# Attention matmuls over all 128 rows of the array, and a third of w_spatial converted after attention

## The chip, the core and the metric

One core of a Trainium2 chip runs the whole kernel. The core has a matrix engine (TensorE; PE in the profile, its weight loads PEld), VectorE (DVE), ScalarE (ACT), GpSimd (POOL) and SyncE (SP), which issues most of the transfers. The engines run side by side, each through its own list of instructions in order, and wait for each other by semaphores. The metric is the device time of the kernel in microseconds (us).

## The reference

Two parts follow each other: a chunked attention, and a gated network whose gate mixes tokens. There are 4 batches, 8 heads, 768 tokens and 64 elements a head. Each chunk of 32 queries sees 8 memory keys and a window of 56 keys around it, 64 keys in all.

```python
for c in range(nc):                       # 24 chunks of 32 queries
    l_start = max(0, c_start - 16); r_end = min(S, c_end + 8)
    k_full = concatenate([mem_k, k[:, :, l_start:r_end]])
    v_full = concatenate([mem_v, v[:, :, l_start:r_end]])
    scores = scale * (q_c @ k_full.T)
    a = softmax(scores)
    out[:, :, c_start:c_end] = a @ v_full

x = out                                   # (4, 768, 512)
h = relu(x @ w_in)                        # 512 -> 1024
u, v = h[..., :512], h[..., 512:]
v_n = (v - mean(v)) / sqrt(var(v) + 1e-6)
v_s = einsum('ts,bsd->btd', w_spatial, v_n) + b_spatial
out = (u * v_s) @ w_out
```

## The kernel before

**Planner.** Each step is handed to `op` (line 40) with its engine, an assumed duration, what it reads and writes, and a rank. `Plan.order` (line 64) lays the steps out in an assumed time: of the steps that could start first, the lowest rank goes first. Each engine gets its steps in that order, and keeps to it on the chip. Names such as `big`, `st`, `uo` are rings of buffers; a new user waits until the oldest one's last reader is done. Transfers on SP wait in their order too.

**Attention.** A unit is 4 chunks (128 queries) of all 8 heads of a batch, 24 units in all, 6 a batch. Heads come in pairs: head pair t (four of them) has its first head (r = 0) in rows 0 to 63 of the 128 partitions and its second (r = 1) in rows 64 to 127, since a head has 64 elements. For unit i, `prep` (line 366, copy at 368) copies the keys on ACT from the loaded tile into one of two buffers `kmain`, in slots of 40 columns, where the last 8 hold the memory keys (`spread_keys`, line 372, on POOL at the start of each batch). `burst` (line 379) is a run of small matmuls on PE, all issued in line 382: for unit i the scores of queries and keys, and for unit i - 1 probabilities times values. For each head pair, chunk and head there is one matmul with 64 rows, 32 columns of weights (the queries of a chunk, or its probabilities) and 64 columns streamed. It occupies a tile of 64 by 32 of the array, so that eight matmuls of different tiles can be under way at once. The profile counts each of these 32-bit matmuls as two instructions, and as many weight loads. The result is the tile `sx`, two PSUM banks. After that follow the row maximum, subtraction, exponential and sum (`softmax`, line 425), the transpose of the probabilities (line 466), their copy `pT` (469), and for the unit before it the normalisation `xs` (418), its transpose `xt` (481) and the split into a high and a low part `x` (486, 490). Values lie in `vmain` (three unit buffers), with rows of memory values written by `spread_mem` (line 353). The last `x` carries the key `attended` (line 495).

**Input product.** `ffn_v` and `ffn_u` multiply `x` and `w_in`, both split in a high and a low part, by three matmuls each (lines 519 to 521). Their steps have later ranks than attention, so they fill PE between the bursts. Results go to DRAM (`vn_far`, `u_far`). `w_in` and `w_out` come as 64-bit numbers and are turned into 32-bit ones by `from_f64` (line 803: ACT 814 and 819, DVE 823 and 824, POOL 829).

**Second half.** `spatial` and `ffn_o` use seven products in place of eight (`product`, line 627, matmuls in line 679). For this `right_hand` (line 856) builds seven blocks of a weight matrix from its quarters: sums on POOL (line 871), high parts on ACT (843), low parts on POOL or DVE (847). `w_sp_pair(s)` (line 897) loads two row blocks of `w_spatial` into the ring `big` (four buffers) and builds one third of `wsp`. The three thirds are made during attention, at units 6, 10 and 14; the bias at unit 16. `w_out_pair` (line 886) loads `w_out` into the same ring with a rank of 200, and its blocks are built once the input product is done. The memory of attention is given back by `second_half` (line 596), when the first tile of the second half is made, and that of `w_in` by `third_part` (line 603).

Of the kernel before, what the change touches and what calls it, by code (L numbers as in the profile page):

```python
# [140 lines left out]
def tile_chunked_attention_gmlp(  # L141
# [68 lines left out]
    wsp = const.tile([P, 7, 2, HU, HT], F32R, name="wsp")  # L210
# [22 lines left out]
    vmain = values.tile([P, T, NV * UC, D], F32, name="vmain")  # L233
    NK = sizes["kT"]
    kmain = [values.tile([P, T, UC + 1, SLOT], F32, name=f"kmain{j}") for j in range(NK)]
    make_identity(nc, ident)
    nc.vector.memset(mhalf, -0.5)
# [79 lines left out]
    def v_of(i):  # L317
        o = (i % NV) * UC
        return vmain[:, :, o:o + UC]

    def load_v(i, seq=True, second="SP"):
        b, c0 = i // UB, (i % UB) * UC
        n = UC
        v4 = v_of(i).rearrange("p t c d -> p t (c d)")
        for r in range(2):
            p0 = r * D
# [26 lines left out]
    def spread_mem(i, eng, rank):  # L353
        b, o = i // UB, (i % NV) * UC
        for r in range(2):
            rows = slice(r * D + CH, r * D + SLOT)

            def spread(rows=rows):
                to, of = vmain[rows, :, o:o + UC], memv[rows, b].unsqueeze(2).broadcast_to([M, T, UC, D])
                if eng == "ACT":  # L360
                    nc.scalar.copy(to, of)
                else:
                    {"DVE": nc.vector, "POOL": nc.gpsimd}[eng].tensor_copy(to, of)
            op(eng, 2.6 if eng == "POOL" else 1.25, spread, r=[("memv", r)], w=[("vmem", i % NV, r)], rank=rank)

    def prep(i, rank):
        def keys():
            nc.scalar.copy(kmain[i % NK][:, :, :, 0:CH], k_of(i).rearrange("p t (c s) -> p t c s", s=CH))  # L368

        op("ACT", act(T * (UC + 1) * CH), keys, r=qk_keys(i, "k"), w=[("kmain", i % NK)], rank=rank)  # L370

    def spread_keys(i, rank):
        b = i // UB

        def spread():
            nc.gpsimd.tensor_copy(kmain[i % NK][:, :, 0:UC, CH:SLOT], memT[:, b].unsqueeze(2).broadcast_to([P, T, UC, M]))
        op("POOL", 0.3, spread, r=["memT"], w=[("kmem", i % NK)], rank=rank)

    def burst(i, rank, split=False):
# [4 lines left out]
        def go(what):  # L384
            if ("sx", i) not in t_:
                alloc("sx", i, [P, 2, 2, T, D], F32, psum=True)
            sx = t_["sx", i]
            tiles = [(t, c, r, slice(r * D, (r + 1) * D)) for t in range(T) for c in range(UC) for r in range(2)]
            if "s" in what:
                tq = q_of(i)  # L390
                kT = kmain[i % NK].rearrange("p t c s -> p t (c s)")
                for t, c, r, rows in tiles:
                    mm(sx[c * CH:(c + 1) * CH, r, 0, t], tq[rows, t, c * CH:(c + 1) * CH],
                       kT[rows, t, c * SLOT:c * SLOT + WIN])
            if "a" in what:
                pT, vt = t_["pT", i - 1], v_of(i - 1)
                for t, c, r, rows in tiles:
                    mm(sx[c * CH:(c + 1) * CH, r, 1, t], pT[rows, t, c * CH:(c + 1) * CH], vt[rows, t, c])
        whole = ("a" if i >= 1 else "") + ("s" if i < NU else "")
        for what in (whole if split else [whole]):  # L400
            reads, writes = [], []
            us = 0.4
            if "s" in what:
                reads += qk_keys(i, "q") + [("kmain", i % NK), ("kmem", i % NK)]
                writes.append(("sx", i, 0))
                us += 0.6
            if "a" in what:
                reads += [("pT", i - 1)] + v_keys(i - 1)
                writes.append(("sx", i, 1))
                us += 0.7  # L410
            op("PE", us, lambda what=what: go(what), r=reads, w=writes, rank=rank, tail=0.25)
        if i >= 1:
            j = i - 1

            def norm():
                xs = alloc("xs", j, [P, T, 2, D], F32)
                rec = t_["rec", j]
                nc.vector.tensor_tensor(xs.rearrange("p t r d -> p r t d"), t_["sx", i][:, :, 1],  # L418
                                        rec.rearrange("p t r -> p r t").unsqueeze(3).broadcast_to([P, 2, T, D]),
                                        op=ALU.mult)  # L420
# [4 lines left out]
    def softmax(i, rank):  # L425
        c0 = (i % UB) * UC

        def top():
            s = t_["sx", i][:, :, 0]
# [4 lines left out]
            mx = t_["mx", i] = small.tile([P, 2, T], F32, tag="mx", name="mx")  # L434
            nc.vector.tensor_reduce(mx, s, axis=AX.X, op=ALU.max)

        def sub():
            p = alloc("p", i, [P, T, 2, WIN], F32)
            nc.vector.tensor_tensor(p.rearrange("p t r w -> p r t w"), t_["sx", i][:, :, 0],
                                    t_["mx", i].unsqueeze(3).broadcast_to([P, 2, T, WIN]), op=ALU.subtract)  # L440
# [155 lines left out]
    def second_half():  # L596
        if "op" not in sb:
            attention.close()
            for name in ("vr", "op", "sm"):
                sb[name] = pool(name, bufs=sizes[name], side="right")  # L600
            ps["y"] = pool("ps_y", bufs=sizes["y"], space=PSUM, side="right")
# [106 lines left out]
    def spatial(b):  # L708
# [4 lines left out]
        def done(name, p, bank):  # L713
# [37 lines left out]
            elif name == "p3":  # L751
# [3 lines left out]
                lambda i, x, s: wsp[:, i, x, s], lambda i: [("wsp", s, i) for s in range(HU)], "DVE", True, done)  # L755
# [47 lines left out]
    def from_f64(name, src_, rank, load_rank, home):  # L803
# [7 lines left out]
        load(get, src_.bitcast(U32).rearrange("p (c w) -> p c w", w=2), w=[("big", big)], rank=load_rank, seq=True)  # L811
# [74 lines left out]
    def w_out_pair(c, rank, load_rank):  # L886
# [6 lines left out]
        (zu, ku), (zd, kd) = [from_f64(("wout", d), w_out[d * P:(d + 1) * P], rank, load_rank, True) for d in (c + 2, c)]  # L893
        end = [("fin", n) for n in range(count[0])]
        right_hand("wout", c, HN, halves(zu), halves(zd), [ku, *end], [kd, *end], dst, rank, "POOL", "DVE")

    def w_sp_pair(s, rank):
        raw = []
# [9 lines left out]
        right_hand("wsp", s, HT, u, d, ku, kd, lambda i, x: wsp[:, i, x, s], rank, "POOL", "POOL")  # L908


    def load_bias(rank):
# [7 lines left out]
        op("POOL", 0.8, clear, r=[("wsp", 2, 6)], w=[raw], rank=rank)  # L919
# [37 lines left out]
    for i in range(NU + 1):  # L957
# [13 lines left out]
        if i in (UB, UB + 4, UB + 8):  # L971
            w_sp_pair((i - UB) // 4, 10.0 * i + 15)
        if i == UB + 10:
            load_bias(10.0 * i)
    for b in range(B):
        for hf in range(2):
            for tt in range(hf * HU, (hf + 1) * HU):
                ffn_v(b, tt)
            for d in range(ND):
                ffn_u(b, hf, d)  # L980
    for c in range(2):
# [61 lines left out]
```

## Time and profile before

| | |
|---|---|
| three runs | 398.49, 399.73, 404.72 us; median 399.73 |
| the profiled execution | 404.88 us, its span 403.0 us |
| busy in the span | PE 365.8, PEld 334.4, DVE 272.7, ACT 190.7, POOL 151.8 us |
| mean granted clock of TensorE | 0.979 |
| instructions | 11801, of them 4972 matmuls and 4972 weight loads |

The span runs from the first to the last instruction of one execution. Busy time counts an engine's instructions, not its waits. In the rows of groups, after the bar stand the busy time in us, the mean time of one instruction in ns, and the idle time of the engine just before them with what ended it; "issue" means that the profile shows nothing that the engine waited for. In the timeline a row is the start, the length and the instruction, and idle time before it in brackets.

### The profile page before, as it was taken

How to read it: one execution, taken by the hardware profiler on the slowest of the kernel's cores; microseconds unless marked ns; L12 is line 12 of the kernel's file. 1: busy time of each engine (PE TensorE's matmuls, PEld its weight loads, DVE VectorE, ACT ScalarE, POOL GpSimd, SP SyncE). 2: the span in 40 equal slices, each digit the busy share in tenths (PEclk: the TensorE clock that was granted, in tenths of full speed). 3: DMA queues.
4: the chain of work that ended last, by engine and by line, in shares of the span. 5: the costliest groups of instructions: out<-in, count | busy, mean ns of one | idle time of the engine just before them, and what ended most of it. 6: DMA issues, size and time to landing. Idle time of an engine off the chain costs nothing.

```text
span 403.0 us, 11801 instructions
## 1 busy us (share of the span) xinstructions
PE 365.8 (91%) x4972; PEld 334.4 (83%) x4972; DVE 272.7 (68%) x462; ACT 190.7 (47%) x344; POOL 151.8 (38%) x151
## 2 busy tenths in 40 slices
PE   1587588799799999899999999999999999999986
PEld 0365478689689888698897989999999999999976
DVE  3577975376468676585859559967956884788473
ACT  4546544363346364253456234728344734453271
POOL 5323643561269058440113218560136033403510
PEclk9998889899989999999999999999999999999999
DMA  7987767835693877646582443832640544041004
GB/s 213 249 218 211 199 177 207 262 99 174 195 250 116 252 219 221 173 138 193 152 258 108 160 156 124 283 116 96 219 153 6 157 171 144 5 167 67 0 2 156
DMA packets 47368, 65.12 MB, mean 162 GB/s; under 512 B 4434, under 2 KB 38866, under 8 KB 47316
## 3 DMA queue, kind: packets, MB, share of 16 engines
q1 hardware_dynamic: 46900, 64.25, 52.6%
q8 instruction: 39, 0.64, 0.7%
q10 hardware_dynamic: 416, 0.13, 0.1%
q14 instruction: 13, 0.11, 0.1%
HBM read 45.49 MB, written 18.87 MB: 160 GB/s over the span
## 4 chain that ended last, share of the span: by engine, by line
PE 73%; DMA 9%; DVE 7%; issue 5%; ACT 3%; SPq 0%; ACTq 0%; DVEq 0%
PE y L679 20%; PE f L679 15%; PE f L519 9%; PE f L520 8%; PE f L521 8%; PE sx L382 7%; DMA k<-in_k_dram 3%; PE xt L481 3%; PE pt L466 2%; DMA big<-in_moe_w_in_dram 1%; PE f L534 1%; DMA big<-in_moe_w_out_dram 1%; DVE st L569 1%; DMA q<-in_q_dram 1%; DMA big<-in_moe_w_spatial_dram 1%
## 5 line engine op out<-in xcount | busy, mean ns | idle before, releaser
L735 POOL TENSOR_TENSOR ug<-st,ug 128x384 f32<-128x384 f32 x32 | 43.2, 1363 | 87.0 <-DVE st L727 67.7
L679 PE MATMUL y<-wsp,op 128*128 128x384 f32 x288 | 52.6, 336 | 0.0
L679 PEld LDWEIGHTS y<-wsp,op 128*128 128x128 f32 x288 | 50.2, 188 | 0.0
L519 PE MATMUL f<-win_h,x 128*128 128x512 f32 x96 | 43.6, 454 | 3.4 <-issue 2.2
L519 PE MATMUL f<-x,win_h 128*128 128x384 f32 x128 | 46.0, 359 | 0.0
L521 PE MATMUL f<-x,win_h 128*128 128x384 f32 x128 | 43.3, 339 | 0.0
L520 PE MATMUL f<-x,win_l 128*128 128x384 f32 x128 | 43.3, 338 | 0.0
L565 POOL TENSOR_TENSOR rstd<-ve,mhalf 128x1 f32<-128x1 f32 x24 | 15.8, 659 | 72.4 <-DVE ve L561 68.3
L679 PE MATMUL f<-wsp,op 128*128 128x384 f32 x216 | 40.1, 336 | 0.0
L657 DVE TENSOR_TENSOR op<-sm,op 128x768 fp32r<-128x768 f32 x32 | 31.8, 997 | 11.6 <-ACT op L654 11.5
L520 PE MATMUL f<-win_h,x 128*128 128x512 f32 x96 | 39.5, 412 | 0.0
L521 PE MATMUL f<-win_l,x 128*128 128x512 f32 x96 | 39.3, 409 | 0.0
L654 ACT CAST op<-sm 128x768 fp32r<-128x768 f32 x32 | 26.4, 838 | 26.3 <-DVE sm L641 14.4
L679 PE MATMUL y<-wout,op 128*128 128x256 f32 x288 | 36.2, 280 | 1.5 <-DVE op L657 1.0
L679 PEld LDWEIGHTS f<-wsp,op 128*128 128x128 f32 x216 | 37.5, 188 | 0.0
L418 DVE TENSOR_TENSOR xs<-sx,rec 128x512 f32<-128x512 f32 x24 | 16.5, 687 | 30.4 <-PE sx L382 30.4
L679 PEld LDWEIGHTS y<-wout,op 128*128 128x128 f32 x288 | 34.8, 188 | 2.1 <-DVE op L657 1.4
L382 PEld LDWEIGHTS sx<-kmain,q 64*32 64x32 f32 x1536 | 18.0, 112 | 20.5 <-issue 13.4
L382 PE MATMUL sx<-kmain,q 64*32 64x64 f32 x1536 | 22.3, 238 | 13.1 <-ACT kmain L368 6.7
L382 PE MATMUL sx<-vmain,pT 64*32 64x64 f32 x1536 | 24.0, 230 | 8.6 <-issue 5.1
L382 PEld LDWEIGHTS sx<-vmain,pT 64*32 64x32 f32 x1536 | 20.1, 108 | 11.2 <-issue 6.7
L721 ACT COPY st<-y 128x384 f32<-128x384 f32 x32 | 15.4, 480 | 28.0 <-PE y L679 27.7
(91 smaller groups left out, 754.9 us busy)
## 6 DMA issues: line engine op xcount, KB each, us to landing
vmain<-in_v_dram SPq DMA_DIRECT2D x48, 128.0 KB
vn_far<-st SPq DMA_DIRECT2D x24, 256.0 KB
u_far<-uo SPq DMA_DIRECT2D x32, 192.0 KB
vr<-vn_far SPq DMA_DIRECT2D x8, 768.0 KB
ug<-u_far SPq DMA_DIRECT2D x16, 384.0 KB
q<-in_q_dram SPq DMA_DIRECT2D x11, 512.0 KB
out_dram<-ot SPq DMA_DIRECT2D x36, 128.0 KB
vmain<-in_v_dram SPq DMA_DIRECT2D x47, 96.0 KB
```

What stands on the lines that cost most here:

```text
L382: nc.tensor.matmul(o, w_, m, start=True, stop=True, skip_group_check=True)
L418: nc.vector.tensor_tensor(xs.rearrange("p t r d -> p r t d"), t_["sx", i][:, :, 1], rec.rearrange("p t r -> p r t").unsqueeze(3).broadcast ...
L481: nc.tensor.transpose(a[:, t], xs[:, t], ident)
L519: nc.tensor.matmul(o, lh, rh, start=(j == 0), stop=False)
L520: nc.tensor.matmul(o, ll, rh, start=False, stop=False)
L521: nc.tensor.matmul(o, lh, rl, start=False, stop=(j == len(pairs) - 1))
L565: nc.gpsimd.tensor_tensor(a, t_["ve", i], mhalf, op=ALU.pow)
L654: nc.scalar.copy(half(0), of())
L657: nc.vector.tensor_tensor(half(1), of(), half(0).bitcast(F32), op=ALU.subtract)
L679: nc.tensor.matmul(o, x, y, start=first and m == 1 and not (seed and bank != "x"), stop=m == 3 * chunks, skip_group_check=True)
L721: op("ACT", act(HT), lambda: nc.scalar.copy(alloc("st", st(x)[1], [P, HT], F32), t_[bank]), r=[bank], w=[st(x)], rank=rank)
L735: nc.gpsimd.tensor_tensor(g, t_[st(x)], g, op=ALU.mult)
```

## The change

The two heads of a pair are computed by one matmul over all 128 rows. For this `kmain` and `vmain` get a new dimension of two and become twice as large. Rows 0 to 63 hold the keys (values) of the first head in the first half and zeros in the second; rows 64 to 127 hold zeros in the first half and the second head's in the second. So one matmul with 128 rows and 32 columns of weights streams 128 columns and gives 64 results of each head. A unit's products take 32 matmuls in the program in place of 64. The zeros are written once at the start: two fills of `kmain` on POOL, one before and one after the identity, and three of `vmain` on DVE, ahead of `mhalf`, which ACT's warm-up reads. The key copy on ACT becomes two copies of 64 rows, and the copy of the memory keys on POOL becomes two as well. `sx` has its scores in one bank and the attention's result in the other, no longer one bank for each head of a pair; the steps that read it keep their sizes.

The larger buffers take the room of a third of `wsp`. That third gets a tile of its own, `wsp_end`, in the memory that attention leaves. Its rows are loaded at rank 205 into `big`, and its conversion waits for `attended`. The other two thirds are made at units 6 and 13, and the bias's clearing waits for the second. The loads of `w_out` now wait for the high part of the fourth block of the last third.

```diff
-    wsp = const.tile([P, 7, 2, HU, HT], F32R, name="wsp")
+    wsp = const.tile([P, 7, 2, HU - 1, HT], F32R, name="wsp")
...
-    vmain = values.tile([P, T, NV * UC, D], F32, name="vmain")
+    vmain = values.tile([P, T, 2, NV * UC, D], F32, name="vmain")
     NK = sizes["kT"]
-    kmain = [values.tile([P, T, UC + 1, SLOT], F32, name=f"kmain{j}") for j in range(NK)]
+    kmain = [values.tile([P, T, 2, UC + 1, SLOT], F32, name=f"kmain{j}") for j in range(NK)]
+    nc.gpsimd.memset(kmain[0], 0.0)
+    for j in range(NV):
+        nc.vector.memset(vmain[:, :, :, j * UC:(j + 1) * UC], 0.0)
     make_identity(nc, ident)
+    nc.gpsimd.memset(kmain[1], 0.0)
     nc.vector.memset(mhalf, -0.5)
...
     def prep(i, rank):
-        def keys():
-            nc.scalar.copy(kmain[i % NK][:, :, :, 0:CH], k_of(i).rearrange("p t (c s) -> p t c s", s=CH))
-
-        op("ACT", act(T * (UC + 1) * CH), keys, r=qk_keys(i, "k"), w=[("kmain", i % NK)], rank=rank)
+        for r in range(2):
+            rows = slice(r * D, (r + 1) * D)
+
+            def keys(r=r, rows=rows):
+                nc.scalar.copy(kmain[i % NK][rows, :, r, :, 0:CH], k_of(i)[rows].rearrange("p t (c s) -> p t c s", s=CH))
+            n = T * (UC + 1) * CH
+            op("ACT", act(n), keys, r=qk_keys(i, "k"),
+               w=[("kmain", i % NK, r)], rank=rank)
...
         def spread():
-            nc.gpsimd.tensor_copy(kmain[i % NK][:, :, 0:UC, CH:SLOT], memT[:, b].unsqueeze(2).broadcast_to([P, T, UC, M]))
-        op("POOL", 0.3, spread, r=["memT"], w=[("kmem", i % NK)], rank=rank)
+            for r in range(2):
+                rows = slice(r * D, (r + 1) * D)
+                nc.gpsimd.tensor_copy(kmain[i % NK][rows, :, r, 0:UC, CH:SLOT],
+                                      memT[rows, b].unsqueeze(2).broadcast_to([D, T, UC, M]))
+        op("POOL", 0.6, spread, r=["memT"], w=[("kmem", i % NK)], rank=rank)
...
-                alloc("sx", i, [P, 2, 2, T, D], F32, psum=True)
+                alloc("sx", i, [P, 2, T, 2, D], F32, psum=True)
             sx = t_["sx", i]
-            tiles = [(t, c, r, slice(r * D, (r + 1) * D)) for t in range(T) for c in range(UC) for r in range(2)]
+            tiles = [(t, c, slice(c * CH, (c + 1) * CH)) for t in range(T) for c in range(UC)]
             if "s" in what:
                 tq = q_of(i)
-                kT = kmain[i % NK].rearrange("p t c s -> p t (c s)")
-                for t, c, r, rows in tiles:
-                    mm(sx[c * CH:(c + 1) * CH, r, 0, t], tq[rows, t, c * CH:(c + 1) * CH],
-                       kT[rows, t, c * SLOT:c * SLOT + WIN])
+                kT = kmain[i % NK].rearrange("p t r c s -> p t r (c s)")
+                for t, c, rows in tiles:
+                    mm(sx[rows, 0, t], tq[:, t, rows], kT[:, t, :, c * SLOT:c * SLOT + WIN])
             if "a" in what:
                 pT, vt = t_["pT", i - 1], v_of(i - 1)
-                for t, c, r, rows in tiles:
-                    mm(sx[c * CH:(c + 1) * CH, r, 1, t], pT[rows, t, c * CH:(c + 1) * CH], vt[rows, t, c])
+                for t, c, rows in tiles:
+                    mm(sx[rows, 1, t], pT[:, t, rows], vt[:, t, :, c])
...
+            t_["wsp"] = pool("wsp_end", bufs=1, side="right").tile([P, 7, 2, HT], F32R, name="wsp_end")
...
-        (zu, ku), (zd, kd) = [from_f64(("wout", d), w_out[d * P:(d + 1) * P], rank, load_rank, True) for d in (c + 2, c)]
+        (zu, ku), (zd, kd) = [from_f64(("wout", d), w_out[d * P:(d + 1) * P], rank, load_rank, True, [("wsp", HU - 1, 3, "h")]) for d in (c + 2, c)]
...
+    def w_sp_at(i, x, s):
+        if s < HU - 1:
+            return wsp[:, i, x, s]
+        second_half()
+        return t_["wsp"][:, i, x]
+
     def w_sp_pair(s, rank):
+        end = ["attended"] if s == HU - 1 else []
...
-        right_hand("wsp", s, HT, u, d, ku, kd, lambda i, x: wsp[:, i, x, s], rank, "POOL", "POOL")
+        right_hand("wsp", s, HT, u, d, ku + end, kd + end, lambda i, x: w_sp_at(i, x, s), rank, "POOL", "POOL")
...
-        op("POOL", 0.8, clear, r=[("wsp", 2, 6)], w=[raw], rank=rank)
+        op("POOL", 0.8, clear, r=[("wsp", 1, 6)], w=[raw], rank=rank)
...
-        if i in (UB, UB + 4, UB + 8):
-            w_sp_pair((i - UB) // 4, 10.0 * i + 15)
+        if i in (UB, UB + 7):
+            w_sp_pair((i - UB) // 7, 10.0 * i + 15)
...
+    w_sp_pair(HU - 1, 205.0)
     for c in range(2):
         w_out_pair(c, 260.0, 200.0)
```

More of the change, by code (lines that the diff above doesn't have):

```diff
@@ L318, in v_of @@
         o = (i % NV) * UC
-        return vmain[:, :, o:o + UC]
+        return vmain[:, :, :, o:o + UC]
     def load_v(i, seq=True, second="SP"):
@@ L323, in load_v @@
         n = UC
-        v4 = v_of(i).rearrange("p t c d -> p t (c d)")
         for r in range(2):
+            v4 = v_of(i)[:, :, r].rearrange("p t c d -> p t (c d)")
             p0 = r * D
@@ L356, in spread_mem, with spread @@
             rows = slice(r * D + CH, r * D + SLOT)
-            def spread(rows=rows):
-                to, of = vmain[rows, :, o:o + UC], memv[rows, b].unsqueeze(2).broadcast_to([M, T, UC, D])
+            def spread(rows=rows, r=r):
+                to, of = vmain[rows, :, r, o:o + UC], memv[rows, b].unsqueeze(2).broadcast_to([M, T, UC, D])
                 if eng == "ACT":
@@ L403, in burst @@
             if "s" in what:
-                reads += qk_keys(i, "q") + [("kmain", i % NK), ("kmem", i % NK)]
+                reads += qk_keys(i, "q") + [("kmain", i % NK, 0), ("kmain", i % NK, 1), ("kmem", i % NK)]
                 writes.append(("sx", i, 0))
@@ L417, in norm @@
                 rec = t_["rec", j]
-                nc.vector.tensor_tensor(xs.rearrange("p t r d -> p r t d"), t_["sx", i][:, :, 1],
-                                        rec.rearrange("p t r -> p r t").unsqueeze(3).broadcast_to([P, 2, T, D]),
-                                        op=ALU.mult)
+                nc.vector.tensor_tensor(xs, t_["sx", i][:, 1], rec.unsqueeze(3).broadcast_to([P, T, 2, D]), op=ALU.mult)
             op("DVE", dve(512), norm, r=[("sx", i, 1), ("rec", j)], w=[("xs", j)], rank=rank - 0.5)
@@ L428, in top @@
         def top():
-            s = t_["sx", i][:, :, 0]
+            s = t_["sx", i][:, 0]
             if c0 == 0:
@@ L433, in top @@
                 nc.vector.memset(s[P - CH:P, :, :, WIN - M:WIN], NEG)
-            mx = t_["mx", i] = small.tile([P, 2, T], F32, tag="mx", name="mx")
+            mx = t_["mx", i] = small.tile([P, T, 2], F32, tag="mx", name="mx")
             nc.vector.tensor_reduce(mx, s, axis=AX.X, op=ALU.max)
@@ L438, in sub @@
             p = alloc("p", i, [P, T, 2, WIN], F32)
-            nc.vector.tensor_tensor(p.rearrange("p t r w -> p r t w"), t_["sx", i][:, :, 0],
-                                    t_["mx", i].unsqueeze(3).broadcast_to([P, 2, T, WIN]), op=ALU.subtract)
+            nc.vector.tensor_tensor(p, t_["sx", i][:, 0], t_["mx", i].unsqueeze(3).broadcast_to([P, T, 2, WIN]), op=ALU.subtract)
         def exp():
@@ L754, in spatial @@
         return product("s", b, ["p1", "p2", "p6", "p5", "p7", "p4", "p3"], [quarter(0, 0), quarter(0, 1), quarter(1, 0), quarter(1, 1)], HU, 2 * P, 2, HT,
-                lambda i, x, s: wsp[:, i, x, s], lambda i: [("wsp", s, i) for s in range(HU)], "DVE", True, done)
+                lambda i, x, s: w_sp_at(i, x, s), lambda i: [("wsp", s, i) for s in range(HU)], "DVE", True, done)
     def ffn_o(b):
@@ L801, in ffn_o, with from_f64 @@
                 lambda i, x, d: t_["wout"][:, i, x, d], lambda i: [("wout", d, i) for d in range(2)], "DVE", False, done)
-    def from_f64(name, src_, rank, load_rank, home):
+    def from_f64(name, src_, rank, load_rank, home, after=()):
         big = ("big", *name)
@@ L810, in get @@
             return a
-        load(get, src_.bitcast(U32).rearrange("p (c w) -> p c w", w=2), w=[("big", big)], rank=load_rank, seq=True)
+        load(get, src_.bitcast(U32).rearrange("p (c w) -> p c w", w=2), w=[("big", big)], r=after, rank=load_rank, seq=True)
         def scale_():
```

## Prediction

> **What bounds the kernel now.** I read the page first, then a table by stretches, then the timeline of TensorE (PE) around the attention matmuls. The table's columns are the stretch, its length, the busy time of PE, PEld, DVE, ACT and POOL, the granted clock, the DMA share and GB/s.
>
> ```profile
> span 403.0 us, 11801 instructions
> PE 365.8 (91%) x4972; PEld 334.4 (83%) x4972; DVE 272.7 (68%) x462; ACT 190.7 (47%) x344; POOL 151.8 (38%) x151
> ```
> ```profile
> 0.00:61.60 61.60, 38.06 (x808) 29.37 (x808) 40.84 (x76) 31.15 (x54) 26.39 (x33) 0.92 0.78 211
> 61.60:222.60 161.00, 152.67 (x3008) 132.44 (x3007) 106.17 (x212) 75.69 (x135) 67.09 (x73) 0.98 0.64 187
> 222.60:246.70 24.10, 24.10 (x141) 22.42 (x129) 14.07 (x25) 8.74 (x15) 7.34 (x9) 1.00 0.43 156
> 246.70:403.00 156.30, 151.01 (x1031) 150.21 (x1029) 111.58 (x152) 75.06 (x142) 51.01 (x38) 1.00 0.35 116
> ```
>
> Until 61.6 us PE is busy for only 38 us: weights arrive and are converted, and the attention units wait for one engine after the other. From there to 222.6 us attention runs between the matmuls of the input product, and PE idles 8.3 of 161 us. Then the rest of the input product follows, and from 246.7 us the spatial and output products. So after 61.6 us the time is PE's work plus PE's idle time, and the change touches both. The timeline of PE (start, length, what, idle time before it) shows a burst of line 382, the same line at half clock, and four stalls; below them stands the page's row of the instruction queue.
>
> ```profile
> 48.09 1.14 PE L382 MATMUL sx<-kmain,q 64*32 64x64 f32 x64
> 71.25 0.86 PE L382 MATMUL sx<-kmain,q 64*32 64x64 f32 x64
> 71.91 0.96 PE L382 MATMUL sx<-vmain,pT 64*32 64x64 f32 x64
> 72.80 0.44 PE L519 MATMUL f<-x,win_h 128*128 128x384 f32 x1
> 73.08 0.34 PE L520 MATMUL f<-x,win_l 128*128 128x384 f32 x1
> 73.25 0.33 PE L521 MATMUL f<-x,win_h 128*128 128x384 f32 x1
> ...
> 32.13 0.42 PE L382 MATMUL sx<-kmain,q 64*32 64x64 f32 x3 [3.82 <-issue]
> 75.77 0.50 PE L519 MATMUL f<-win_h,x 128*128 128x512 f32 x1 [2.19 <-issue]
> 109.78 0.31 PE L382 MATMUL sx<-vmain,pT 64*32 64x64 f32 x6 [2.44 <-issue]
> 170.63 0.30 PE L382 MATMUL sx<-vmain,pT 64*32 64x64 f32 x3 [1.34 <-issue]
> ```
> ```profile
> q8 instruction: 39, 0.64, 0.7%
> ```
>
> A unit's burst is 128 matmuls, each with its weight load: 71.25 to 72.80, 1.55 us, for 256 instructions. All four stalls lie in a burst or just behind one, and "issue" means that no semaphore held PE. The queue row gives 39 packets and 0.64 MB, 16.4 KB each. The program has 4972 matmuls and 4972 weight loads (the page's head), 255 a packet: PE's own instruction stream. So one burst eats one whole packet in 1.6 us, while elsewhere in this stretch a packet lasts several us. I read the stalls as instruction blocks that arrive too late, when a block's edges happen to enclose a burst.
>
> **The change part by part.**
>
> *Bursts.* Counts of line 382 alone, by stretch (PE busy and matmuls, then weight loads), and a chain row for transposes of the same type:
>
> ```profile
> 0.00:61.60 61.60, 11.78 (x704) 9.63 (x704) 0.92 0.78 211
> 61.60:222.60 161.00, 31.31 (x2368) 27.66 (x2368) 0.98 0.64 187
> 94.41 0.44 PE xt L481 x4
> ```
>
> 704 and 2368 matmuls are 5.5 and 18.5 units. After the change a unit issues 64 matmuls and 64 weight loads, but each streams 128 columns through all rows in place of 64 through half of them; four column groups work side by side in place of eight tiles. The transposes stream 128 columns of this type in 0.44/4 = 0.11 us. Per product and column group eight of them follow each other: 8 x 0.11 = 0.88 us. The half-clock row agrees: there 64 columns cost what 128 cost at full clock, and the row is 1.14 us long against 0.86. Two products are 1.76 us, with 0.1 us between and 0.15 us of hand-over as at 72.80 that is 2.0 us against 1.6. The trace holds no such shape, so the ends: 1.76 us if nothing comes between, 2.2 us if the hand-over and the gap double. I take +0.4, from the transposes and the half-clock row: 18.5 x 0.4 = +7.4 us late, and early, where some units run at half clock and PE also idles, 5.5 x 0.5 = +2.8 (0 to 4).
>
> [...]
>
> *Stalls.* A block of 255 instructions can no longer lie inside a burst of 128; the other 127 are transposes and input-product matmuls, which take 0.17 us or more for each matmul with its load (73.08 to 73.25), some 9 us. So the late stalls go: 2.19 + 2.44 + 1.34 = -6.0 us. What is late next is PE itself. They also cost clock:
>
> ```profile
> 31.99:35.40 3.41, 3.27 (x12) 2.61 (x12) 2.78 (x5) 0.99 (x2) 0.34 (x1) 0.50 0.82 268
> 76.36:79.77 3.41, 3.41 (x12) 2.98 (x11) 0.42 (x3) 0.00 (x0) 2.15 (x3) 0.50 0.73 181
> 110.50:113.90 3.40, 3.40 (x12) 2.72 (x11) 2.81 (x7) 1.53 (x3) 1.44 (x3) 0.50 1.03 324
> ```
>
> Behind three of the stalls the clock is 0.50 for 3.4 us, a loss of 1.7 us each: late -3.4. The early one (3.82 + 1.7) lies where other things are late too; I count half, -2.8 (0 to -5.5).
>
> [...]
>
> *Keys, fills, values.*
>
> ```profile
> L368 ACT COPY kmain<-k 128x640 f32<-128x640 f32 x24 | 17.2, 726 | 15.3 <-DMA k<-in_k_dram 12.1 <-PE sx L382 3.2
> 44.17 1.35 ACT L368 COPY kmain<-k 128x640 f32<-128x640 f32 x2
> L376 POOL COPY kmain<-memT 128x128 f32<-128x128 f32 x8 | 2.3, 289 | 12.7 <-PE sx L382 11.0 <-DMA memT<-in_mem_k_dram 1.6
> L917 POOL MEMSET big<- 128x1024 f32 x1 | 1.0, 957 | 0.1
> 0.81 0.06 DVE L237 MEMSET mhalf<- 128x1 f32 x1 [0.81 <-PEq L1016]
> 2.50 0.20 ACT L240 ACTIVATE warm<-mhalf 128x1 f32<-128x1 f32 x1
> 5.91 0.72 ACT L368 COPY kmain<-k 128x640 f32<-128x640 f32 x1 [3.22 <-DMA k<-in_k_dram]
> ```
>
> The key copy becomes two of 64 rows with the same 640 elements a row, each about as long: two in a row took 1.35 us, so +0.63 us of ACT a unit. Late, ACT goes from 75.7 + 11.7 to 87 of 161 us busy and two key buffers let the copy run a unit ahead: nothing; without that cover up to 11.7. Early it lies on the path in part: 6 x 0.63 = 3.8 at most, I take +2. The eight memory-key copies become pairs, 0.3 us more each on POOL, a unit ahead of use: nothing. Masked scores keep their shapes, so softmax and normalisation cost the same.
>
> The fills: DVE writes 3 x 2048 elements a row ahead of `mhalf`, POOL 1600 twice around the identity. At the POOL row's 0.93 ns an element (a DVE fill of that size is not in the trace; half that is the other end) DVE is busy until 0.8 + 5.7 = 6.5 us, and ACT's warm-up, which reads `mhalf`, and the first key copy behind it wait: +0.8 (0 to 1). POOL's 3.0 us end before that. The value loads wait on SP for their fill, with weight loads behind them, 2 us at most and before the first was issued. Together +1.
>
> *The moved third of w_spatial.*
>
> ```profile
> L871 POOL TENSOR_TENSOR big<-big 128x384 f32<-128x384 f32 x12 | 12.1, 1023 | 0.4 <-DMA big<-in_moe_w_spatial_dram 0.4
> L847 POOL TENSOR_TENSOR wsp<-big,wsp 128x768 fp32r<-128x768 f32 x9 | 16.7, 1861 | 7.0 <-ACT wsp L843 6.9
> L824 DVE SCALAR_TENSOR_TENSOR st<-big,st 128x512 uint32<-128x512 uint32 x12 | 9.3, 773 | 0.4
> L823 DVE TENSOR_SCALAR st<-st 128x512 uint32<-128x512 uint32 x12 | 6.3, 529 | 0.8 <-ACT st L814 0.8
> L829 POOL TENSOR_TENSOR big<-st,big 128x512 uint32<-128x512 uint32 x4 | 5.2, 1308 | 12.6 <-ACT st L814 10.6 <-ACT uo L590 1.1 <-issue 0.9
> 226.65 0.69 DVE L490 TENSOR_TENSOR x<-xt,x 128x512 fp32r<-128x512 f32 x1 [0.46 <-ACT x L486]
> 227.00:246.70 19.70, 19.70 (x104) 18.20 (x103) 10.20 (x18) 7.70 (x13) 5.18 (x6) 1.00 0.50 183
> 246.70:273.70 27.00, 27.00 (x157) 27.00 (x156) 21.79 (x26) 13.64 (x26) 18.32 (x14) 1.00 0.53 173
> 273.75 1.45 PE L679 MATMUL y<-wout,op 128*128 128x256 f32 x11
> ```
>
> It starts when attention ends, 227.3 us (the DVE row). One third is 4 x 1.02 + 3 x 1.86 + 1.0 = 10.7 us of POOL. The first spatial product at 246.7 needs only its first block, some 2 us after 227.3, and the later products come 3 us apart: 19 us of input product cover it. But the w_out loads now wait on SP for a conversion of that third, and for the `big` buffers it holds. Behind a waiting load SP holds the stores of `u_far` and `vn_far` and the `vr` loads; two `uo` buffers give ACT, and so PE, a few us. And the first half of w_out's conversion, which ran between 203 and 226 us (POOL's group L829 has its four there), now goes behind: 5.2 us more of POOL. POOL from 227 to 273.7 is then 5.2 + 18.3 + 10.7 + 5.2 = 39.4 of 46.7 us, and the output product wants w_out at 273.75. That just fits; DVE has 32 of 46.7 us there and gets 4 x 1.3 = 5.2 more. I take +1 (0 to +10). What POOL saves before 222 us is worth nothing, as PE was the late one; its other idle time there, 8.3 - 6.0 = 2.3 us, bounds it.
>
> *The sum.* 7.4 + 2.8 - 6.0 - 3.4 - 2.8 + 2 + 1 + 1 = +2.0. The profiled execution took 404.88 us with its 403.0 us span, so it would become 407; the three timed runs have their median at 399.73, 5 us lower, and the same step gives 402.
>
> **The rivals.**
>
> *Faster: bursts close up.* If loads and matmuls pack to 1.76 us (24 x 0.16 = +3.8) and the early stall counts in full (-6.0 - 3.4 - 5.5 = -14.9), with +1 for the start, the sum is -10: 390. For it speaks that the old burst spends time on 256 issues; against it that early units wait for ACT and DMA as well. Chance 0.14.
>
> *Slower: w_out is late.* POOL becomes the bound between 227 and 274. It decides once w_out's last operand passes 274; the spare 7 us are used up if POOL and DVE slow each other. With the full +10 in place of +1 the sum is +11: 411. Against it: POOL was idle half of that stretch. Chance 0.15.
>
> *Slower: the stalls stay*, because they are no instruction fetch or because the matmuls are split again and the stream stays as long: without the -12.2, 414. Against it stand the packet size and the four places. Chance 0.08.
>
> [...] Chance 0.03.
>
> **How the numbers follow.** My forecast, 402, keeps 0.60; its own range is 395 to 409, by the ends of bursts (-5, +4) and the early part (about 3 either way). A measurement of this kernel tells 2% from no change: 392 and 408. Nearly all of the first rival is faster, 0.13, and 0.01 of the forecast: 0.14. The slower three give 0.26, less 0.03 where w_out is only a little late, plus 0.03 from the top of the forecast: 0.26. No change: 0.60. For 8 in 10 the range takes in half of the first rival and the w_out case: 391 to 413.
>
> **What would show it.** The page: x768 for both groups of line 382 with a shape of 128*32, some 27 instruction packets in place of 39, and no "issue" stall over 1 us by a burst after 60 us. [...] Line 368: x48. Line 847's last blocks of wsp behind the end of attention, w_out's conversion ended before the first output product, and PE without a gap there; a gap named POOL or DVE there proves the w_out rival.

## The result, and the profile after

In 20 runs of each, the changed kernel takes 396.0 us (median, 393.7 to 399.05) and the kernel before 401.34 us (397.22 to 404.72); the ratio is 0.9887, 95% interval 0.9856 to 0.9917. So it is 1.1% faster, within the 2% that counted as no change, and on the other side of no change than the forecast (+2 us). The ratio compares the fast runs of the two kernels alone, so it differs a little from the quotient of the medians, which are over all runs. The 396.0 us lies inside the range that was given, 391 to 413 us, but it came about by other steps than those of the sum. The profiled execution took 394.99 us. Its page (head and instruction queue):

```profile
span 393.1 us, 8743 instructions
PE 367.9 (94%) x3436; PEld 334.3 (85%) x3436; DVE 281.2 (72%) x465; ACT 209.8 (53%) x368; POOL 157.4 (40%) x161
q8 instruction: 27, 0.44, 0.5%
```

PE has 1536 matmuls fewer and is busy 2.1 us longer; the instruction stream is 27 packets in place of 39. Next come two tables by stretches, before and after, cut at the same events: the first whole burst (scores and values products together) and the first spatial product. Columns as in the prediction.

```profile
0.00:61.60 61.60, 38.06 (x808) 29.37 (x808) 40.84 (x76) 31.15 (x54) 26.39 (x33) 0.92 0.78 211
61.60:246.60 185.00, 176.67 (x3135) 154.76 (x3135) 120.14 (x236) 84.34 (x150) 74.34 (x81) 0.98 0.61 183
246.60:403.00 156.40, 151.11 (x1032) 150.31 (x1030) 111.68 (x152) 75.16 (x142) 51.11 (x38) 1.00 0.35 117
```
```profile
0.00:57.40 57.40, 39.22 (x465) 28.62 (x465) 47.67 (x80) 36.83 (x62) 32.09 (x42) 1.00 0.82 221
57.40:235.70 178.30, 176.80 (x1945) 154.86 (x1945) 120.40 (x236) 98.15 (x166) 70.41 (x78) 1.00 0.63 190
235.70:393.10 157.40, 151.86 (x1029) 150.85 (x1027) 113.13 (x151) 74.85 (x142) 54.88 (x42) 1.00 0.35 117
```

The early part is 4.2 us shorter (forecast: 3 longer), the middle 6.7 shorter (forecast: 2 shorter), the second half 1.0 longer (as forecast). The profiles differ by 9.9 us and the medians by 5.3, because the profiled execution of before lies 3.5 us above its median and that of after 1.0 below. The timeline of PE after (start, length, what, idle before): the first burst, the second burst of scores and what stands between it and the values products, a whole burst, and the first output product.

```profile
8.95 1.94 PE L393 MATMUL sx<-kmain,q 128*32 128x128 f32 x32 [8.95 <-POOL vmain L367]
...
28.79 1.08 PE L393 MATMUL sx<-kmain,q 128*32 128x128 f32 x32 [0.16 <-ACT kmain L375]
29.80 0.50 PE L526 MATMUL f<-win_h,x 128*128 128x512 f32 x1
30.13 0.39 PE L527 MATMUL f<-win_h,x 128*128 128x512 f32 x1
30.36 0.40 PE L528 MATMUL f<-win_l,x 128*128 128x512 f32 x1
30.83 1.08 PE L393 MATMUL sx<-vmain,pT 128*32 128x128 f32 x32
...
65.33 1.08 PE L393 MATMUL sx<-kmain,q 128*32 128x128 f32 x32
66.23 1.06 PE L393 MATMUL sx<-vmain,pT 128*32 128x128 f32 x32
67.22 0.45 PE L526 MATMUL f<-x,win_h 128*128 128x384 f32 x1
...
262.07 0.68 PE L687 MATMUL y<-wsp_end,op 128*128 128x384 f32 x3
262.59 0.63 PE L687 MATMUL y<-wout,op 128*128 128x256 f32 x4
```

A burst now takes 65.33 to 67.22, 1.89 us, against 1.55 to 1.69 us before (mean 1.61, without the three that a stall interrupts). No issue stall is left by a burst, and the output product follows the spatial one without a gap. The rows for the start, of ACT and of DVE:

```profile
6.09 1.28 ACT L375 ACT_TABLE_LOAD   x1 [6.09 <-DMA k<-in_k_dram]
7.38 1.47 ACT L375 COPY kmain<-k 64x640 f32<-64x640 f32 x2
```
```profile
1.23 1.76 DVE L238 MEMSET vmain<- 128x2048 f32 x1 [1.23 <-PEq L1032]
```

The first burst begins 2.2 us later than before (8.95 against 6.74). The warm-up behind the three fills comes too late to load the table of the activation function, so the table load of 1.28 us, which the kernel before had behind it at 2.48 us, stands between the landed keys and their first copy, and the two copies end at 8.85 us. (The row of the burst names a copy on POOL that ended 0.1 us later; the scores don't read the values that it copies.) And yet the early part is shorter. That is what the experiments had to explain.

### The profile page after: what moved, and what is told of

The parts are those of the page before. It is cut to its first block, busy times and chain, and to the rows that moved or that the text cites. A ratio compares the mean times of both kernels' runs of the same rounds, so it can differ in the third digit from the quotient of the medians.

```text
span 393.1 us, 8743 instructions
## 1 busy us (share of the span) xinstructions
PE 367.9 (94%) x3436; PEld 334.3 (85%) x3436; DVE 281.2 (72%) x465; ACT 209.8 (53%) x368; POOL 157.4 (40%) x161
## 4 chain that ended last, share of the span: by engine, by line
PE 75%; DMA 8%; DVE 7%; ACT 5%; issue 2%; POOL 2%; ACTq 0%; DVEq 0%; SPq 0%; POOLq 0%
PE y L687 20%; PE f L687 15%; PE f L526 9%; PE f L528 9%; PE f L527 9%; PE sx L393 9%; DMA k<-in_k_dram 3%; PE xt L488 2%; PE pt L473 2%; DMA memv<-in_mem_v_dram 1%; DMA vmain<-in_v_dram 1%; DMA big<-in_moe_w_in_dram 1%; ACT kmain L375 1%; DMA u_far<-uo 1%; POOL wsp L855 1%
## 5 line engine op out<-in xcount | busy, mean ns | idle before, releaser
L375 ACT COPY kmain<-k 64x640 f32<-64x640 f32 x48 | 34.8, 724 | 17.9 <-DMA k<-in_k_dram 13.5
L526 PE MATMUL f<-win_h,x 128*128 128x512 f32 x96 | 41.1, 428 | 0.0
L527 PE MATMUL f<-win_h,x 128*128 128x512 f32 x96 | 38.0, 396 | 1.3 <-DVE x L497 1.3
L687 PE MATMUL y<-wsp,op 128*128 128x384 f32 x192 | 39.0, 339 | 0.0
L528 PE MATMUL f<-win_l,x 128*128 128x512 f32 x96 | 37.8, 394 | 0.0
L393 PE MATMUL sx<-kmain,q 128*32 128x128 f32 x768 | 27.2, 284 | 9.7 <-POOL vmain L367 9.0
L393 PEld LDWEIGHTS sx<-kmain,q 128*32 128x32 f32 x768 | 20.6, 113 | 16.6 <-issue 15.1
L687 PEld LDWEIGHTS y<-wsp,op 128*128 128x128 f32 x192 | 34.1, 188 | 0.0
L687 PE MATMUL f<-wsp,op 128*128 128x384 f32 x144 | 29.1, 338 | 0.0
L597 ACT ACTIVATE uo<-f 128x384 f32<-128x384 f32 x32 | 15.7, 492 | 23.1 <-PE f L528 14.7
L393 PE MATMUL sx<-vmain,pT 128*32 128x128 f32 x768 | 26.4, 279 | 1.7 <-ACT pT L476 1.2
```

The lines of the kernel that those rows point to most:

```text
L375: nc.scalar.copy(kmain[i % NK][rows, :, r, :, 0:CH], k_of(i)[rows].rearrange("p t (c s) -> p t c s", s=CH))
L393: nc.tensor.matmul(o, w_, m, start=True, stop=True, skip_group_check=True)
L526: nc.tensor.matmul(o, lh, rh, start=(j == 0), stop=False)
L527: nc.tensor.matmul(o, ll, rh, start=False, stop=False)
L528: nc.tensor.matmul(o, lh, rl, start=False, stop=(j == len(pairs) - 1))
L597: op("ACT", act(HT), lambda: nc.scalar.activation(alloc("uo", i, [P, HT], F32), t_["f", n], AF.Relu), r=[("f", n)], w=[("uo", i)], rank=rank)
```

## The experiments

Line numbers shift a little from kernel to kernel; the burst is the line with `sx`. Where an expectation numbers a place in PE's stream, it counts matmuls, loads and PE's own semaphore instructions in the trace. Counted so, the four stalls of before stand at 704, 2241, 3521 and 5824, that is at 192 or 193 above a multiple of 256. **Theory A**: the gain is the stalls that the shorter stream no longer has. **A2**, formed later: two causes, the block edges and a new order of the early units, which the planner makes because a unit's keys are now two steps. Letters that stand for rivals are told in the expectations.

**The merged matmuls split again.** The changed kernel, each merged matmul as two of 64 columns, over all 128 rows still.

```diff
-    mm(sx[rows, 0, t], tq[:, t, rows], kT[:, t, :, c * SLOT:c * SLOT + WIN])
+    for r in range(2):
+        mm(sx[rows, 0, t, r], tq[:, t, rows], kT[:, t, r, c * SLOT:c * SLOT + WIN])
...
```

> The changed kernel, but each matmul of a burst is split into two that stream 64 columns each over all 128 rows (one per head). The array streams as many columns as in the changed kernel, the two key copies, the zero fills and the moved third of w_spatial stay, and PE's instruction stream is as long as that of the kernel before (4972 matmuls, 39 instruction packets). Theory A (the gain is that instruction blocks no longer run dry): stalls of 1 to 4 us named issue come back, at multiples of 256 instructions, some with a half clock behind them, and the time is 402 to 408 us, 1.5 to 3% over the changed kernel's 396. Theory B (the gain comes from the moved third or from the order of the early part): the time stays at 395 to 398 us.

It took 402.4 us, 1.0005 of before (0.9967 to 1.0042): the gain is gone. The timeline of PE of this kernel:

```profile
71.47 0.41 PE L393 MATMUL sx<-vmain,pT 128*32 128x64 f32 x5 [0.84 <-issue]
...
106.02 1.12 PE L393 MATMUL sx<-kmain,q 128*32 128x64 f32 x62
...
108.07 0.50 PE L528 MATMUL f<-win_h,x 128*128 128x512 f32 x1
```

But the stalls that came back are small, two of 0.85 us without a half clock behind them; the bursts became longer too, 2.05 us (106.02 to 108.07) and up to 2.27. That costs 0.2 to 0.4 us 24 times, the larger part of the loss. The time fits theory A, its mechanism only in part.

**Only the moved third.** The kernel before, and of the change only `wsp_end` and what hangs on it.

```diff
...
-        if i in (UB, UB + 4, UB + 8):
-            w_sp_pair((i - UB) // 4, 10.0 * i + 15)
+        if i in (UB, UB + 7):
+            w_sp_pair((i - UB) // 7, 10.0 * i + 15)
...
+    w_sp_pair(HU - 1, 205.0)
```

> The kernel before with only the second part of the change: the last third of w_spatial is converted after attention, the other two at units 6 and 13, and w_out's loads wait for it. Bursts, key copies and fills are as before. Theory A: PE was the late engine before 222 us, so the time is that of the kernel before within 1% (398 to 404 us), and the stalls at multiples of 256 instructions are there, in the same or other bursts. Theory B: 394 to 398 us, most of the change's gain.

401.67 us, 0.9962 (0.9911 to 1.0012). The third is worth nothing, or a little.

**The warm-up ahead of the fills.** The changed kernel, with `mhalf`, `eps` and `warm` set before `vmain` is filled.

```diff
+    nc.vector.memset(mhalf, -0.5)
...
+    nc.scalar.activation(warm, mhalf, AF.Exp)
     nc.gpsimd.memset(kmain[0], 0.0)
...
```

> The changed kernel with mhalf, eps and the ACT warm-up ahead of the zero fills. In the changed kernel's trace ACT's table load of 1.28 us stands between the landing of the first keys (6.04 us) and their copy (7.38 us), and the first burst starts at 8.95 us. Theory C1 (the early part is on the path that sets the end): the first burst starts at about 7.6 us and the time falls by 1.0 to 1.5 us (0.3%). Theory C2 (the early part waits for weights anyway): the first burst is earlier by as much and the time is the same within 0.15%.

399.19 us, 0.9897 (0.9834 to 0.996): no gain over the changed kernel. The timeline of PE, and a row of the table by stretches:

```profile
7.62 1.94 PE L393 MATMUL sx<-kmain,q 128*32 128x128 f32 x32 [7.62 <-ACT kmain L375]
...
29.52 2.07 PE L541 MATMUL f<-win_h 128*128 128x512 f32 x4 [4.98 <-ACT win_h L851]
```
```profile
28.60:32.00 3.40, 2.48 (x7) 1.99 (x8) 2.22 (x5) 3.35 (x6) 0.00 (x0) 0.50 0.76 243
```

The first burst did come 1.33 us earlier. Then PE waited 4.98 us for the converted weights, and the clock was 0.50 behind it. In this execution a gain at the very start is lost within 22 us.

**Thirty-two instructions more.** The kernel before, with four of the twelve matmuls of `keep_warm` (line 527) issued in five pieces each. Same columns and same work, but everything behind them moves by 32 instructions.

```diff
-    nc.tensor.matmul(o, win_h[:, c, DH:DH + P], win_h[:, c, DH:], start=True, stop=True)
+    for n0, n1 in ((0, 128), (128, 256), (256, 384), (384, 448), (448, 512)) if c == 0 else ((0, DH),):
+        nc.tensor.matmul(o[:, n0:n1], win_h[:, c, DH:DH + P], win_h[:, c, DH + n0:DH + n1], start=True, stop=True)
```

> The kernel before, with nothing of the change: four of the twelve warming matmuls (512 columns each) are issued as five pieces each, so that 32 more instructions with the same streamed columns precede the bursts, and each 256-instruction block ends 32 instructions earlier in the work. In the trace of before the four issue stalls lie at instruction 704, 2241, 3521 and 5824, all 192 or 193 over a multiple of 256. From that trace, with blocks ending 32 earlier, no block lies wholly in a burst; at most two stalls of 1 us are left, near 107 and 139 us. Theory A: the time falls to 390 to 396 us, as much as the change or more, since bursts keep their 1.6 us. Theory B: 400 to 403 us, as before.

398.3 us, 0.9892 (0.9841 to 0.9942): as much as the whole change, from a shift, though short of theory A's 390 to 396 us. The timeline of PE shows the one issue stall of before that is left and another wait inside a burst, and the table by stretches a half clock that no issue stall precedes:

```profile
103.02 0.42 PE L382 MATMUL sx<-vmain,pT 64*32 64x64 f32 x22 [0.39 <-issue]
139.56 1.09 PE L382 MATMUL sx<-vmain,pT 64*32 64x64 f32 x64 [2.15 <-ACT pT L469]
```
```profile
48.00:51.40 3.40, 1.33 (x66) 1.12 (x57) 2.37 (x4) 1.39 (x3) 1.58 (x3) 0.50 0.86 215
```

So the stalls do belong to edges of 256 instructions that enclose a burst: the program's work is the same and all issue stalls by a burst but 0.39 us are gone. The wait of 2.15 us is for ACT's copy of the probabilities and stands at no edge; it and the half clock behind it are a part of what theory A missed. But the first whole burst began at 61.57 us, as before (61.67), though the early stall of 3.82 us was gone too. The 4.2 us of the early part have another cause.

**The old bursts in the changed kernel.** Everything as after, the order of all engines too, but 64-row matmuls as before (4972 again); `sx` has its old layout, and the steps that read it follow.

```diff
-    for t, c, rows in tiles:
-        mm(sx[rows, 0, t], tq[:, t, rows], kT[:, t, :, c * SLOT:c * SLOT + WIN])
+    for t, c, rows, r, hr in tiles:
+        mm(sx[rows, r, 0, t], tq[hr, t, rows], kT[hr, t, r, c * SLOT:c * SLOT + WIN])
...
```

> The changed kernel in everything (fills, two key copies, moved third, and with them the planner's order on every engine), but the bursts as before: 128 matmuls of 64 rows and 64 columns for a unit on the diagonal blocks, so 4972 matmuls and 39 instruction packets. Theory A1 (blocks that run dry are the whole gain): the stalls come back as often as in the kernel before, and the time is 400 to 404 us. Theory A2 (two causes: the dry blocks, and an order on the engines that leaves PE less idle and no half clock before 60 us): the early part is that of the changed kernel (the first whole burst near 57.5 us, not 61.7), bursts take 1.6 us against 1.88 (24 x 0.28 = 6.7 us less), stalls of about 3 us in all come back at 192 over a multiple of 256 instructions, the largest near instruction 2240, with up to 2 us of half clock: 393 to 397 us.

396.27 us, 0.9903 (0.9853 to 0.9953), beside the changed kernel again on the same chip:

> The changed kernel once more, on the chip and beside the runs of the other two, to have their distance to it: 394 to 399 us, 0.986 to 0.992 of the kernel before.

394.17 us, 0.9859 (0.9803 to 0.9916). Most of the gain is there without a merged matmul, with this left in the timeline of PE:

```profile
28.98 1.34 PE L544 MATMUL f<-win_h 128*128 128x512 f32 x4 [3.52 <-ACT win_h L854]
...
35.29 0.32 PE L393 MATMUL sx<-vmain,pT 64*32 64x64 f32 x8 [0.90 <-issue]
...
72.45 0.31 PE L393 MATMUL sx<-vmain,pT 64*32 64x64 f32 x5 [2.29 <-issue]
```

The stalls are as A2 expected, and no half clock follows the late one. The early part is not: the first whole burst, expected near 57.5 us, began at 61.01. In this execution PE waited 3.52 us for converted weights, with half clock behind the wait, where the changed kernel waited 1.25 us in the same place. PE's order is the same in both, so the order alone does not secure the early gain.

**Scores and values products apart.** The kernel with the old bursts, where every unit's burst is two steps (as in the first units), so that other matmuls can lie between them.

```diff
-        attend(i, 10.0 * i, 1 <= i < UB)
+        attend(i, 10.0 * i, 1 <= i < NU)
```

> As the run before (all of the change but the merged matmuls), and the scores and the values' product of a unit are two steps on PE for every unit, as they are in both kernels for the first batch; input-product matmuls can stand between. Then 128 instructions of a burst are followed by others, and no block of 256 lies in a burst. Theory A: no issue stall over 0.5 us after 60 us; each split costs another hand-over of about 0.25 us, 18 x 0.25 = 4.5 us; 391 to 397 us. If the stalls had another cause than the block's length, they stay, and the time is 398 or more.

419.18 us, 1.0464 (1.0382 to 1.0546): wrong by far. The timeline of PE:

```profile
80.06 0.34 PE L393 MATMUL sx<-kmain,q 64*32 64x64 f32 x14 [4.57 <-issue]
...
288.06 0.39 PE L690 MATMUL y<-wout,op 128*128 128x256 f32 x1 [2.67 <-ACT op L665]
```

The first spatial product began at 238.6 us, no later than without the edit (238.86), but the first output product at 283.1 in place of 265.5: the planner had laid out the second half anew as well, and PE waits there for ACT and DVE. Splitting didn't remove the stalls either. One edit to a step's form changes the order of all engines to the end; this was the hint to test the order by itself.

**Only the two key copies.** The kernel before, with the key copy of a unit as two steps of 64 rows each (and the memory keys' assumed 0.6 us). No zeros, no merged matmuls, no moved third.

```diff
-        op("ACT", act(T * (UC + 1) * CH), keys, r=qk_keys(i, "k"), w=[("kmain", i % NK)], rank=rank)
+        for r in range(2):
...
+            op("ACT", act(T * (UC + 1) * CH), keys, r=qk_keys(i, "k"), w=[("kmain", i % NK, r)], rank=rank)
...
```

> The kernel before, in which only the key copy is two copies of 64 rows in place of one of 128: no zeros, no merged matmuls, no moved third, no fills. By that the planner issues the first units on PE in the same order as in the changed kernel. Theory A2 (two causes: the new order of the early units, and no stalls at block edges): the first whole burst begins some 4 us earlier than the 61.67 us of before, at 57 to 58 us plus what one stall costs there; late stalls stay at counts of 192 modulo 256; 396 to 399 us. Rival A1 (the early gain came from the absent stalls alone, the order is worth nothing): first whole burst 61 to 63 us, time within 0.4% of before. Rival C (the two copies cost ACT time early, as forecast, +2 us): 1.005 times before.

396.27 us, 0.9799 (0.9742 to 0.9856), at the lower end of what A2 expected, and clear of both rivals. First whole burst at 58.29 us; late stalls of 2.00 and 1.00 us, at counts of 2240 and 4544.

**Eight instructions more**, in the kernel with the old bursts and in the one with two key copies, by warming matmuls in two pieces as above.

> The changed kernel with the old bursts of 64 rows, and four of the twelve warming matmuls issued in two pieces each, the same columns in all: 8 more instructions of PE ahead of the attention's bulk, so that the old edges of the instruction blocks fall at other places of the bursts. Theory A2: no stall over 1 us at a block edge, bursts 1.60 us in place of 1.88, so 24 x 0.28 = 6.7 us less than the changed kernel if nothing else ends last, less what remains of stalls: 390 to 394 us, under the changed kernel. Rival (the old bursts run dry at any place of the edges, the sum of the stalls only moves): 396 to 399 us, as with the old bursts unshifted.

> The kernel before with the two key copies and the 8 shifted instructions: no zeros, no merged matmuls, no moved third. If the change's gain comes from the order of the early units and from the place of the block edges (A2), this has both: 390 to 395 us, the same as the changed kernel or under it. If the merged matmuls or the moved third have a gain of their own: 398 us or more.

396.07 us, 0.981 (0.9758 to 0.9862), and 397.01 us, 0.9819 (0.9755 to 0.9882). Both lie above the ranges that A2 gave, the first in that of its rival, and neither is faster than the kernel with two copies on the same chip. In the first the stall at count 2240 stayed; it now leaves nine matmuls of the burst behind it in place of five. Eight instructions were too few to free that edge:

```profile
69.08 0.32 PE L393 MATMUL sx<-vmain,pT 64*32 64x64 f32 x9 [2.11 <-issue]
```

In the second no late stall of over 0.6 us was left, against 2.00 and 1.00 us with the two copies alone; an interval of 0.6% to either side is too wide to show these 3 us.

**Only the order.** As the two key copies, but the first of the two steps issues nothing and the second the one copy of 128 rows. PE and DVE get the same list as there; what the chip computes is the kernel before.

```diff
-        def keys():
...
+        for r in range(2):
+            def keys(r=r):
+                if r:
+                    nc.scalar.copy(kmain[i % NK][:, :, :, 0:CH], k_of(i).rearrange("p t (c s) -> p t c s", s=CH))
...
```

> The kernel before, in which the planner is given two steps for a unit's key copy, each with the whole assumed duration, while the chip gets the one copy of 128 rows as before, issued by the second step. Nothing else: only the order in which the engines get their steps is that of the kernel with two copies. If the gain of that kernel (396.27 us, 0.9799 of before) is the new order, as theory A2 says: 0.975 to 0.985 of before, the first whole burst at 57 to 59 us. If two shorter copies have a gain of their own (the first half of the rows is ready earlier): 0.99 to 1.00.

> The changed kernel again, on the chip of the order kernel, for a direct comparison: by A2 the merged matmuls give back what the absent block-edge stalls bring, so the two are within 0.7% of each other; if the merged matmuls have a gain of their own on top of the order, this one is 1% or more lower.

394.11 us, 0.9723 (0.9652 to 0.9794), and the changed kernel beside it 394.82 us, 0.9783 (0.9728 to 0.9839). A step that exists only in the planner's list (with the memory keys' assumed 0.6 us) gives the whole gain. Here is the table by stretches of the order kernel, its instruction queue, and its timeline of PE:

```profile
0.00:56.00 56.00, 37.48 (x817) 27.75 (x817) 41.69 (x77) 31.09 (x53) 28.38 (x36) 0.97 0.83 222
56.00:230.90 174.90, 171.50 (x3129) 151.59 (x3129) 122.39 (x237) 84.75 (x151) 70.78 (x78) 1.00 0.66 196
230.90:386.70 155.80, 150.61 (x1029) 149.81 (x1027) 110.12 (x150) 75.06 (x142) 50.21 (x38) 1.00 0.35 118
```
```profile
q8 instruction: 39, 0.64, 0.7%
```
```profile
26.17 0.86 PE L384 MATMUL sx<-kmain,q 64*32 64x64 f32 x64 [0.48 <-ACT kmain L370]
26.96 0.50 PE L521 MATMUL f<-win_h,x 128*128 128x512 f32 x1
...
27.97 1.03 PE L384 MATMUL sx<-vmain,pT 64*32 64x64 f32 x64
...
67.83 0.30 PE L384 MATMUL sx<-vmain,pT 64*32 64x64 f32 x3 [1.96 <-issue]
```

And the same place in the timeline of before:

```profile
26.83 0.82 PE L382 MATMUL sx<-vmain,pT 64*32 64x64 f32 x60
...
27.51 0.80 PE L382 MATMUL sx<-kmain,q 64*32 64x64 f32 x58
```

Before, the values products of unit 1 came first and the scores of unit 2 right behind, as one run of 128 matmuls; a block edge hit its last three, and those scores were complete only after the stall that the prediction quotes, at 32.5 us. In the new order the scores of unit 2 come first, at 26.17 (28.79 in the changed kernel), with three input-product matmuls between them and the values products, and are complete at 27.0. On DVE the row maximum of unit 2 starts at 27.06 us in place of 33.19 and its subtraction at 32.04 in place of 34.85, and the first whole burst comes 5.7 us earlier. The stream is as long as before, 39 packets. The order also moved the edges: of the three late stalls only the first is left, with 1.96 us, and two of under 0.6 us stand at other edges.

## Why the prediction was wrong

**Keys: the step that failed.** It counted the second key copy as work on ACT (+2 us early, nothing late) and took the order of the steps as given. The second copy is also a second step in the list from which the planner lays out every engine. With this (and the longer time assumed for the copy of the memory keys) and no instruction of the chip added, the kernel runs at 0.9723 (0.9652 to 0.9794) of before. I had described that the planner works with assumed durations and did not ask what it would do with a longer one. On PE the rows above show the first unit where it matters.

**The early part, +3 forecast, -4.2 measured.** Bursts +2.8, keys +2, start +1 and half of a stall, -2.8, were summed over a fixed order. The start was worse than said: 2.2 us in place of 0.8, through the table load, though the fill itself was as estimated (1.76 us against 1.9). An earlier start by 1.33 us brought nothing in the warm-up experiment, so it cost little. And the half clocks before 60 us did not all come from the early stall: the shifted kernel had the stall removed and half clock from 44.6 to 54.8 us.

**Bursts, +0.4 forecast, +0.28 measured** (1.88 against a mean of 1.61): the right mechanism, a size off; 24 x 0.12 = 2.9 us too much. The two products of a burst start 0.90 us apart (65.33 and 66.23), against 0.88 in the sum; 32 matmuls one behind the other at the transposes' 0.11 us would take 3.5 us. It is not the 1.76 us of bursts that close up, nor twice the 1.61 us of before: here giving up the tiles of 64 rows made a burst 1.17 times as long.

**Late stalls and their clock, -9.4: right in size, in part by luck.** The profile after has neither. The shifted kernel shows what they are: edges of 256 instructions that enclose a burst. But the shorter stream was not needed for most of it: with the changed kernel's order and the old bursts, one late stall of 2.29 us was left and no late half clock. The sum for the middle with the measured burst is 18.5 x 0.28 - 9.4 = -4.2, measured -6.7; six matmuls of the input product fewer lie in that stretch (3135 - 18.5 x 128 = 767 against 1945 - 18.5 x 64 = 761), 1 us of the rest. PE's idle time there fell from 8.33 to 1.50 us, 0.9 us more than the 5.97 us of stalls.

**The moved third, +1 forecast: right in size.** The second half is 1.0 us longer, w_out was ready, and alone the third is 0.9962 (0.9911 to 1.0012).

**The merged matmuls themselves bring nothing that these runs can tell**: 394.82 us with them, 394.11 without, on the same chip and with the same order on PE for the first 100 us (behind that the moved third changes it). In the two profiles the changed kernel's middle part is 3.4 us longer than the order kernel's: 18.5 x 0.28 = 5.2 us of longer bursts, less the 1.96 us stall. The profile of the order kernel is the lowest of its six executions, so its 386.7 us span flatters it.

**The rivals.** None of the four came true: bursts did not close up to 1.76 us; w_out was in time (262.07 and 262.59 stand without a gap; whether POOL and DVE slow each other was not tried); the stalls went; and the bursts, which the chance of 0.03 had doubled, went from 1.61 to 1.88 us, and no run shows a rule by which they should double. Each of the rivals kept the order fixed, as the forecast did.

**What stays open.** Which of the order's moves does most was not tried one by one; on PE it is both an earlier start of units and other places of the block edges. The early gain also depends on when weights are ready. The first whole burst began at 56.0 to 58.3 us in seven of ten profiles with the new order, but at 60.54 with the merged matmuls split again, at 61.01 with the old bursts, behind the wait of 3.52 us, and at 62.55 with the earlier warm-up, behind that of 4.98. A part of the gain is then a matter of where edges fall, and may go otherwise in a kernel of another length.

## What to carry to other kernels

Where a planner lays out the engines, an edit that splits a step or changes its assumed duration is two edits: compare the order of issue before and after first, and test the order by itself with a step that issues nothing. Where short matmuls run in bursts, count the stream and look where its issue stalls stand: in the kernels here those of over 0.8 us in a burst or shortly behind one stood at 192 or 193 above a multiple of 256 instructions, where a burst of 256 instructions in 1.55 us had used up its block before the packet of the next had landed, and moving the stream by 32 instructions gained as much as the rewritten burst with all that came with it.

## What the runs showed of the hardware

All issue stalls of over 0.8 us that interrupt a burst or stand shortly behind one, in eight kernels, are at 192 or 193 above a multiple of 256 instructions of PE, whatever the kernel had ahead of them; the longest took 4.57 us. The transfers in the trace show the late block itself. The instruction queue moves one packet of 16 KB for each edge, 39 in the kernel before and 27 in the changed one. In the kernel before, the packets of the four edges landed at 30.80, 74.42, 108.48 and 169.01 us, and PE went on at 32.13, 75.77, 109.78 and 170.63, that is 1.3 to 1.6 us later. At every other edge PE came 2.2 us or more after its packet, and in the changed kernel 6.3 us or more. A packet started from 4.8 us before to 4.9 us after PE passed the edge before its own, so about one block ahead. No run shows what sets this distance. Moving the stream by 32 instructions was worth 1.1%. And two merged streams of 64 columns cost less than two separate ones over the same rows: 1.88 us a burst against 2.05 to 2.27.

Small matmuls overlap. In the kernel before the trace has the 64 of the scores at 71.25 us in 0.86 us, each of them 0.21 to 0.24 us long; in the changed kernel the 32 at 65.33 us take 1.08 us, each of them 0.27 to 0.30 us. At a granted clock of 0.50 (76.36 to 79.77 us in the kernel before) input-product matmuls of 384 columns started 0.32 us apart, against 0.17 at full clock.
